# The sinks' share of windowed attention: two float32 products a pair of heads, or one float32r product in high and low parts

## The chip, the cores and the metric

One core of a Trainium2 chip runs the whole program; times are device microseconds (us). Five engines work side by side and meet through semaphores: TensorE (PE, with its weight loads PEld), VectorE (DVE), ScalarE (ACT), GpSimd (POOL) and SyncE (SP), which issues most DMAs. Each runs its own instructions in order. The metric is the time of one execution; the median of 3 runs of the kernel before is 604.55 us (604.28 to 604.63).

## The reference, cut to what matters

```python
# B, H, S, D = 2, 8, 768, 64;  n_sink = 4, window = 128
scores = scale * q @ k.T                       # per batch and head
keep = (key < n_sink) | (0 <= query - key < window)
a = softmax(where(keep, scores, -1e9))
x = (a @ v)  ->  [B*S, H*D] = [1536, 512]      # this is the attention
x = gate1(x @ w_in1) @ w_out1                  # 512 -> 2048 -> 512
x = gate2(x @ w_in2) @ w_out2
```

A query sees the 128 keys of its window and the first 4 keys of the sequence, the sinks. Results are wanted in float32.

## The kernel before, in words

The kernel first computes the attention and then the two feed-forward layers. `GROUPS` cuts the 1536 rows into four groups of (chunk, batch, first query block, number of blocks): (0,0,0,4), (1,0,4,2), (1,1,0,2), (2,1,2,4). Each group is gone through for 4 pairs of heads, which makes 16 pairs of 2 or 4 *units* (a unit is one block of 128 queries for both heads of the pair, 48 in all).

`score` multiplies q and k into PSUM (`ps_s`, L435), DVE adds the mask and takes the row's extreme (L448), ACT takes the exponential and its sum (`sm`, L484). `normalise` runs once for two units: DVE forms 1/sum (L459, L460), copies the normalised columns of the sinks into `psk` (L462; only where the sinks lie outside the window, which is so in 16 of the 24 calls), and GpSimd (L475), ACT (L477) or DVE (L479) scale the rest of `p`. `turn` transposes `p` on TensorE (L520, L521) and ACT or DVE copy it to `pt`. `sinks` transposes `psk` (L527, into `ps_k`) and DVE multiplies it by `own` into `pts` (L530), so that every block of queries keeps only its own rows. `mix` multiplies `v` with `pt` into `ps_v` (L562), for each block of keys and for both heads of the pair by turns, and in 12 of the 16 pairs adds the sinks' part: `vs` with `pts`, one float32 product for each head, last in the sum. ACT and DVE then split the sum into a high and a low part (`xh`, `xl`), since the layers that follow work in float32r with three products (high*high, high*low, low*high).

The order of the steps is written out in the list `steps`: two scores, then the two transposes of the units scored 4 units earlier, `sinks` at a pair's end and its `mix` two units later. `defer(fn, n)` puts work n steps later. PE and SP follow the program's order; on DVE and ACT a scheduler orders by priority before the run. `begin` issues the loads of the first three pairs, clears `vs`, `own` and `psk` on GpSimd and then loads `vs` from DRAM (`load_sinks`, L408): 16 DMAs of 4 KB, since `vs` holds the sinks' rows once for each of 4 query blocks (32 rows a block, 4 rows of the first head, 4 of the second). While the attention runs, pieces of the first layer's weights (float64 in DRAM) are already narrowed on DVE and ACT, and in three places the first products of the layer (`h_group`, L699) stand between attention steps.

Of the kernel before, what the change touches and what calls it, by code (L numbers as in the profile page):

```python
# [63 lines left out]
def sink_columns(n_sink):  # L64
    return n_sink + n_sink % 2


def f32(ap):
    return ap.bitcast(F32)
# [3 lines left out]
def sink_attention_moe_moe_kernel(  # L73
# [44 lines left out]
    def defer(fn, slots=1):  # L118
        waiting.append((clock[0] + slots, fn))
# [209 lines left out]


    NS = sink_columns(n_sink) if fast else 0
    KB = P + NS
    steps = []

# [11 lines left out]
    def build_fast_attention(at_p):  # L346
# [49 lines left out]
            qk[j] = (tq, tk)  # L396

        SR = P // NQ
        vs = at_p.tile([P, B, DM], F32, name="vs", bufs=1)
        pts = [at_p.tile([P, NQ, P], F32, name=f"pts{n}", bufs=1) for n in range(2)]  # L400
        psk = [at_p.tile([P, NQ, SR], F32, name=f"psk{n}", bufs=1) for n in range(DIST)]
        own = at_p.tile([P, NQ], F32, name="own", bufs=1)

        def load_sinks():
            for b in range(B):
                for e in range(2):
                    for r in range(e * NS, P, SR):
                        nc.sync.dma_start(  # L408
                            out=vs[r:r + NS, b, :].rearrange("s (h e d) -> s h e d", e=2, d=D)[:, :, e, :],
                            in_=v[b, 0:NS, :].rearrange("s (h e d) -> s h e d", e=2, d=D)[:, :, e, :],  # L410
                        )
# [13 lines left out]
        def score(j, u):  # L425
            b, i0, nq, first, nb = geom(pairs[j][0])
            tq, tk = qk[j]
            i = i0 + u
            w = widths[min(i, 2)]
            c0 = key_column(max(i - 1, 0)) - key_column(first)  # L430
            banks = []
            for e in range(2):
                rows = slice(e * D, (e + 1) * D)
                banks.append(ps_h.tile([P, 512], F32, tag="h", name="ps_s")[:, :w])
                nc.tensor.matmul(  # L435
                    banks[e], tq[rows, u * P:(u + 1) * P], tk[rows, c0:c0 + w], start=True, stop=True
                )
            if u % 2 == 0:
                two[j] = (
                    at_p.tile([P, 4, 2 * KB], F32, tag="p", name="p", bufs=DIST // 2 + 2),  # L440
                    at_p.tile([P, 4], F32, tag="nm", name="nm", bufs=DIST // 2 + 2),
                    at_p.tile([P, 4], F32, tag="sm", name="sm", bufs=DIST // 2 + 2),
                )
            p4, nm, sm = two[j]
            v = 2 * (u % 2)
            p = p4[:, v:v + 2, :w]
            for e in range(2):
                nc.vector.tensor_tensor_reduce(  # L448
                    out=p[:, e, :], in0=banks[e], in1=masks[min(i, 2)], scale=-SCALE, scalar=BIG,
                    op0=ALU.add, op1=ALU.min, accum_out=nm[:, v + e:v + e + 1],  # L450
                )
                bal.add("dve", 230 + w / 0.96)
            probs[j, u] = p
            if u == nq - 1:
                qk.pop(j)
                defer(lambda: load(j + 3))

            def normalise():
                nc.vector.tensor_scalar_add(out=sm, in0=sm, scalar1=1e-9)  # L459
                nc.vector.reciprocal(out=sm, in_=sm)  # L460
                if w > 2 * P:
                    nc.vector.tensor_tensor(  # L462
                        out=psk[j % DIST][:, u - 1:u + 1, 0:2 * NS].rearrange("p u (e s) -> p u e s", e=2),
                        in0=p4[:, :, P:KB].rearrange("p (u e) s -> p u e s", e=2),
                        in1=sm.rearrange("p (u e) -> p u e", e=2).unsqueeze(3).to_broadcast([P, 2, 2, NS]), op=ALU.mult,
                    )
                end = units.index((j, u)) >= len(units) - 4
                for x in (u - 1, u):
                    for e in range(2):
                        c = 2 * (x % 2) + e  # L470
                        px, r = probs[j, x][:, e, :], sm[:, c:c + 1]
                        if w > 2 * P:
                            px = p4[:, c].rearrange("p (n k) -> p n k", k=KB)[:, :, 0:P]
                        if c < (1 if end else 3):
                            nc.gpsimd.tensor_scalar_mul(out=px, in0=px, scalar1=r)  # L475
                        elif bal.pick(act=190 + w / 1.2, dve=150 + w / 1.4) == "act":
                            nc.scalar.activation(out=px, in_=px, func=AF.Copy, scale=r)  # L477
                        else:
# [12 lines left out]

            defer(expo)
# [31 lines left out]
        def sinks(j, us, nq):  # L524

            ps = bank("ps_k")[:, 0:P]
            nc.tensor.transpose(ps, psk[j % DIST].rearrange("p u s -> p (u s)"), ident)  # L527
            shape = [P, nq - us, P]
            with tc.high_priority(URGENT):
                nc.vector.tensor_tensor(  # L530
                    out=pt[j][1][:, us:nq, :], in0=ps.unsqueeze(1).to_broadcast(shape),
                    in1=own[:, us:nq].unsqueeze(2).to_broadcast(shape), op=ALU.mult,
                )
            bal.add("dve", 140 + (nq - us) * P / 0.96)

        def mix(j):
            gi, hp = pairs[j]
            b, i0, nq, first, nb = geom(gi)
            tv = vv.pop(j)
            ts = vs[:, b, hp * P:(hp + 1) * P]  # L540
            t, tsink = pt.pop(j)
            ps = bank("ps_v")[:, :nq * P]
            us = max(2 - i0, 0)
            sink = us < nq
            ops = [[], []]
            for e in range(2):
                cs = slice(e * D, (e + 1) * D)
                te = t[:, e].rearrange("p n k q -> p (n k q)")
                for kb in range(nb):
                    u = first + kb - i0  # L550
                    u0, u1 = max(u, 0), min(u + 1, nq - 1)
                    c0 = u0 * 2 * P + (P if u >= 0 else 0)
                    c1 = c0 + (u1 - u0 + 1) * P
                    ops[e].append((u0, u1 + 1, tv[:, kb, cs], te[:, c0:c1]))
                o = 0 if i0 == 0 else 1
                ops[e] = ops[e][o::2] + ops[e][1 - o::2]
                if sink:
                    ops[e].append((us, nq, ts[:, cs], tsink[:, us:nq, :].rearrange("p n q -> p (n q)")))
            for n in range(len(ops[0])):
                for e in range(2):  # L560
                    u0, u1, l, r = ops[e][n]
                    nc.tensor.matmul(  # L562
                        ps[e * D:(e + 1) * D, u0 * P:u1 * P], l, r, start=n == 0, stop=n == len(ops[0]) - 1
                    )
            load_v(j + 2)
            n = nq * P
            cs = slice(col0[gi], col0[gi] + n)
            xh, xl = (x_at(0, GROUPS[gi][0], part, hp)[:, cs] for part in "hl")
            with tc.high_priority(URGENT if j >= len(pairs) - 2 else 0):
                high(xh, ps, n, True)  # L570
                low(xl, ps, xh, n)
# [3 lines left out]
        def begin():  # L575
            load(0)
            load_v(0)
            load(1)
            load_v(1)
            load(2)  # L580
            with tc.manual_schedule(engines={mybir.EngineType.Pool}):
                prepare()
                make_identity(nc, ident)
                for t in (vs, own, *psk):
                    nc.gpsimd.memset(t, 0.0)
                for u in range(NQ):
                    nc.gpsimd.memset(own[u * SR:(u + 1) * SR, u:u + 1], 1.0)
            load_sinks()
# [528 lines left out]
```

## Time and profile before

| | |
|---|---|
| median of 3 runs | 604.55 us |
| the profiled execution, its own time | 603.75 us |
| its span, first to last instruction | 602.0 us |
| PE / DVE / ACT / POOL busy in the span | 98 / 78 / 65 / 18 % |
| granted TensorE clock | full in every slice |

A busy engine is one that has an instruction under way. A matmul's recorded time overlaps with that of the next, so what a matmul takes of the engine is read from start to start and not from its length. DVE and ACT overlap a little at the ends of instructions in the same way.

### The profile page before, as it was taken

The numbers are of one execution on the slowest core, as the hardware profiler recorded it, in microseconds if no ns is written. First come the engines' busy times: TensorE is split into PE (matmuls) and PEld (weight loads), VectorE is DVE, ScalarE is ACT, GpSimd is POOL, SyncE is SP. The second block draws the span as 40 slices with busy tenths as digits, with TensorE's granted clock in tenths as the row PEclk, the third lists the DMA queues.
The fourth block names the chain that finished last, engine by engine and source line by source line (L and its number), as shares of the span: only waits on it lengthen the run. The fifth ranks groups of instructions, "written<-read, shape, count | busy, mean of one in ns | idle before, by whom it ended". The sixth has DMA issues, their size and how long they took to land.

```text
span 602.0 us, 8261 instructions
## 1 busy us (share of the span) xinstructions
PE 590.9 (98%) x2872; PEld 473.4 (79%) x2872; DVE 472.3 (78%) x865; ACT 393.8 (65%) x702; POOL 109.5 (18%) x163
## 2 busy tenths in 40 slices
PE   7999899999999999999999999999999999999997
PEld 5666567887888888888888888888888888888885
DVE  5888899799788878577799898897888875666652
ACT  6888897686566665576788785565556545454442
POOL 8676741201011101110000001111011210000000
PEclk9999999999999999999999999999999999999999
DMA  4447713966567676666457105777767555964303
GB/s 143 140 115 243 265 22 106 332 222 225 160 185 235 187 232 180 186 208 234 170 183 271 72 0 175 197 223 212 207 185 235 140 168 152 326 228 139 106 1 140
DMA packets 41786, 107.63 MB, mean 179 GB/s; under 512 B 3728, under 2 KB 13968, under 8 KB 41744
## 3 DMA queue, kind: packets, MB, share of 16 engines
q1 hardware_dynamic: 29872, 72.09, 37.5%
q0 software_dynamic: 11296, 34.61, 18.9%
q8 instruction: 23, 0.38, 0.3%
q10 hardware_dynamic: 576, 0.40, 0.2%
q14 instruction: 19, 0.16, 0.1%
HBM read 69.34 MB, written 35.65 MB: 174 GB/s over the span
## 4 chain that ended last, share of the span: by engine, by line
PE 84%; DVE 7%; ACT 4%; POOL 2%; issue 1%; DMA 1%; POOLq 0%; DVEq 0%
PE ps_y L934 42%; PE ps_h L699 35%; PE ps_v L562 3%; ACT p L484 2%; PE ps_s L435 2%; POOL p L475 1%; DMA wo_d<-w 1%; PE ps_t L521 1%; DVE p L448 1%; PE ps_t L520 1%; DVE w L224 1%; DVE x L773 1%; ACT pt L502 1%; ACT w L198 0%; DVE xt L145 0%
## 5 line engine op out<-in xcount | busy, mean ns | idle before, releaser
L934 PE MATMUL ps_y<-gh,wo 128*128 128x512 f32 x768 | 241.8, 389 | 0.0
L934 PEld LDWEIGHTS ps_y<-gh,wo 128*128 128x128 f32 x768 | 144.2, 188 | 30.0
L934 PE MATMUL ps_y<-gl,wo 128*128 128x512 f32 x384 | 149.8, 390 | 0.3 <-DVE gl L145 0.2
L699 PE MATMUL ps_h<-xh,wi 128*128 128x512 f32 x432 | 140.6, 390 | 0.0
L699 PEld LDWEIGHTS ps_h<-xh,wi 128*128 128x128 f32 x432 | 81.1, 188 | 18.4 <-issue 1.6
L934 PEld LDWEIGHTS ps_y<-gl,wo 128*128 128x128 f32 x384 | 72.1, 188 | 16.4 <-DVE gl L145 1.6
L699 PE MATMUL ps_h<-xl,wi 128*128 128x512 f32 x216 | 84.2, 390 | 0.0
L475 POOL TENSOR_SCALAR p<-p,sm 128x256 f32<-128x256 f32 (+1 forms) x68 | 58.7, 877 | 25.8 <-DVE sm L460 15.7
L699 PE MATMUL ps_h<-xt,st 128*128 128x512 f32 x252 | 61.9, 389 | 0.0
L138 ACT ACTIVATE gh<-r 128x512 fp32r<-128x512 f32 x64 | 40.1, 628 | 29.8 <-PE ps_y L934 27.7
L145 DVE TENSOR_TENSOR gl<-r,gh 128x512 fp32r<-128x512 f32 x64 | 43.8, 689 | 15.7 <-ACT gh L138 15.5
L699 PEld LDWEIGHTS ps_h<-xt,st 128*128 128x128 f32 x252 | 47.2, 188 | 10.0 <-DVE hq L827 0.2
L484 ACT ACTIVATE p<-p,nm 128x260 f32<-128x260 f32 (+2 forms) x96 | 46.3, 484 | 10.8 <-DVE nm L448 10.4
L699 PEld LDWEIGHTS ps_h<-xl,wi 128*128 128x128 f32 x216 | 40.5, 188 | 8.8 <-DVE xl L145 0.4
L448 DVE CUSTOM_DVE_ANT_0 p<-ps_s,mask 128x260 f32<-128x260 f32 (+2 forms) x96 | 35.0, 397 | 6.0 <-PE ps_s L435 5.1
L714 POOL DMA_DIRECT2D h_d<-hq x32 | 18.7, 583 | 114.2 <-ACT xt L138 43.5
L679 ACT ACTIVATE r<-hq,half 128x512 f32<-128x512 f32 x32 | 22.8, 723 | 24.7 <-DVE gl L145 18.8
L272 POOL DMA_DIRECT2D wo_d<-w x16 | 8.6, 537 | 165.3 <-DVE w L224 165.3
L827 DVE TENSOR_TENSOR hq<-ps_h,p 128x512 f32<-128x512 f32 x42 | 28.9, 688 | 10.9 <-PE ps_h L699 10.8
L435 PE MATMUL ps_s<-kraw,qraw 64*128 64x260 f32 (+2 forms) x192 | 32.9, 428 | 4.3 <-DMA kraw<-k_dram 3.2
L680 DVE SCALAR_TENSOR_TENSOR r<-r,hq 128x512 f32<-128x512 f32 x32 | 21.8, 691 | 18.6 <-ACT r L679 18.5
L138 ACT ACTIVATE wo<-w 128x1024 fp32r<-128x1024 f32 (+1 forms) x17 | 17.2, 1009 | 24.4 <-DVE w L224 24.4
(109 smaller groups left out, 949.3 us busy)
## 6 DMA issues: line engine op xcount, KB each, us to landing
h_d<-hq POOLq DMA_DIRECT2D x32, 512.0 KB, 6.1
hq<-h_d SPq DMA_DIRECT2D x32, 512.0 KB
wo_d<-w POOLq DMA_DIRECT2D x16, 512.0 KB, 7.2
raw1i<-moe_w_in_dram SPq DMA_DIRECT2D x8, 1024.0 KB
wr<-wo_d SPq DMA_DIRECT2D x16, 512.0 KB
raw1o<-moe_w_out_dram SPq DMA_DIRECT2D x8, 1024.0 KB
raw0i<-moe_w_in_dram SPq DMA_DIRECT2D x7, 1024.0 KB
raw0o<-moe_w_out_dram SPq DMA_DIRECT2D x7, 1024.0 KB
```

What stands on the lines that cost most here:

```text
L138: nc.scalar.activation(out=dst, in_=src, func=AF.Copy)
L145: nc.vector.tensor_tensor(out=dst, in0=src, in1=f32(hi), op=ALU.subtract)
L435: nc.tensor.matmul(banks[e], tq[rows, u * P:(u + 1) * P], tk[rows, c0:c0 + w], start=True, stop=True)
L448: nc.vector.tensor_tensor_reduce(out=p[:, e, :], in0=banks[e], in1=masks[min(i, 2)], scale=-SCALE, scalar=BIG, op0=ALU.add, op1=ALU.min, a ...
L475: nc.gpsimd.tensor_scalar_mul(out=px, in0=px, scalar1=r)
L484: nc.scalar.activation(out=p[:, e, :], in_=p[:, e, :], func=AF.Exp, scale=-1.0, bias=nm[:, v + e:v + e + 1], accum_out=sm[:, v + e:v + e + 1],
L679: nc.scalar.activation(out=r, in_=h, func=AF.Relu, scale=1.0 / 6.0, bias=half)
L680: nc.vector.scalar_tensor_tensor(out=g, in0=r, scalar=1.0, in1=h, op0=ALU.min, op1=ALU.mult)
L699: nc.tensor.matmul(ps, a[:, kc, :], b[kc], start=start and i == 0, stop=i == len(ops) - 1, skip_group_check=not start,)
L714: nc.gpsimd.dma_start(out=h_d[m][fc // 2][:, e:e + 2, :], in_=t)
L827: nc.vector.tensor_tensor(out=dst, in0=src, in1=p1, op=ALU.add)
L934: nc.tensor.matmul(ys[dm], a[:, cs], b, start=fc == 0 and i == 0, stop=last and i == 2)
```

## The change

For the sinks, `p` and `v` are each split into a high part that float32r holds and the low rest. A head now takes 12 of its 16 rows of a query block's 32: in `psk` they hold p-high, p-low, p-high, in `vs` v-high, v-high, v-low, so that one product over the rows sums the three products. Both heads share one product of 128 columns of weights, put first in the sum of `mix`; the heads' products of `pt` follow, no longer with odd and even key blocks apart. `normalise` writes the sinks to a small tile `pss`, from which DVE makes the parts with two more instructions. `load_sinks` becomes one DMA into a staging tile `vsraw`, and 6 steps later a copy on ACT, a subtraction on DVE, 6 small DMAs from `vsraw` to `vs`, and 3 DMAs that repeat the first 32 rows.

```diff
+    split_sinks = fast and 6 * NS <= P // max(g[3] for g in GROUPS)
...
+        SH = SR // 2
+        SD = F32R if split_sinks else F32
...
+            nc.sync.dma_start(out=flat, in_=v[:, 0:NS, :].rearrange("b s f -> s b f"))
+
+            def split():
+                nc.scalar.activation(out=hi.bitcast(F32R), in_=flat, func=AF.Copy)
+                nc.vector.tensor_tensor(out=lo.bitcast(F32R), in0=flat, in1=hi, op=ALU.subtract)
+                for e in range(2):
+                    for n, part in enumerate((hi, hi, lo)):
+                        r = e * SH + n * NS
+                        nc.sync.dma_start(out=heads(f32(vs[r:r + NS]), e), in_=heads(part, e))
+                for u in range(1, NQ):
+                    nc.sync.dma_start(out=f32(vs[u * SR:(u + 1) * SR]), in_=f32(vs[0:SR]))
+
+            defer(split, 6)
...
+                    t = psk[j % DIST][:, 2 * (u - 1):2 * (u + 1), :]
+                    ts = at_p.tile([P, 4, NS], F32, tag="pss", name="pss", bufs=2) if split_sinks else t[:, :, 0:NS]
                     nc.vector.tensor_tensor(
...
+                        out=ts, in0=p4[:, :, P:KB], in1=sm.unsqueeze(2).to_broadcast([P, 4, NS]), op=ALU.mult
                     )
+                    if split_sinks:
+                        parts = t[:, :, 0:3 * NS].rearrange("p u (n s) -> p u n s", s=NS)
+                        nc.vector.tensor_copy(out=parts[:, :, 0::2, :], in_=ts.unsqueeze(2).to_broadcast([P, 4, 2, NS]))
+                        nc.vector.tensor_tensor(
+                            out=parts[:, :, 1, :], in0=ts, in1=f32(parts[:, :, 0, :]), op=ALU.subtract
+                        )
...
+                if split_sinks:
+                    continue
                 o = 0 if i0 == 0 else 1
                 ops[e] = ops[e][o::2] + ops[e][1 - o::2]
                 if sink:
                     ops[e].append((us, nq, ts[:, cs], tsink[:, us:nq, :].rearrange("p n q -> p (n q)")))
+            whole = sink and split_sinks
+            if whole:
+                nc.tensor.matmul(
+                    ps[:, us * P:nq * P], ts, tsink[:, us:nq, :].rearrange("p n q -> p (n q)"), start=True, stop=False
+                )
```

On TensorE the first `mix` of the program, that of pair 0, stands between transposes and scores. These are the rows of before.

```order
L521 MATMUL ps_t<-ident,p 128x128
L562 MATMUL ps_v<-pt,vraw 64x256 x6
L562 MATMUL ps_v<-pt,vraw 64x128 x2
L562 MATMUL ps_v<-pts_128,vs 64x256 x2
L435 MATMUL ps_s<-kraw,qraw 128x260 x4
```

These are the rows of the change at the same place.

```order
L557 MATMUL ps_t<-ident,p 128x128
L599 MATMUL ps_v<-pts_128,vs 128x256
L605 MATMUL ps_v<-pt,vraw 64x256 x6
L605 MATMUL ps_v<-pt,vraw 64x128 x2
L465 MATMUL ps_s<-kraw,qraw 128x260 x4
```

Two products of the sinks with 64 columns of weights have become one with 128, and the product with `vs` has moved from the end of the `mix` to its head.

On DVE this is the end of pair 0 and the start of pair 1, around the second call of `normalise` (`sm`), before the change.

```order
L448 ISA p,nm<-ps_s,mask_124 128x128
L448 ISA nm 128x1
L459 TENSOR_SCALAR sm<-sm 128x4
L460 RECIPROCAL sm<-sm 128x4
L462 TENSOR_TENSOR psk_130<-p,sm 128x2x8
L479 TENSOR_SCALAR p<-p,sm 128x2x128
L448 ISA p,nm<-ps_s,mask_125 128x256
```

With the change DVE holds these rows there.

```order
L478 ISA p,nm<-ps_s,mask_124 128x128
L478 ISA nm 128x1
L421 TENSOR_TENSOR vsraw<-vsraw 4x1024
L489 TENSOR_SCALAR sm<-sm 128x4
L478 ISA p,nm<-ps_s,mask_125 128x256
L478 ISA nm 128x1
L478 ISA p,nm<-ps_s,mask_125 128x256
L478 ISA nm 128x1
L490 RECIPROCAL sm<-sm 128x4
L540 COPY pt<-ps_t 128x2x128
L494 TENSOR_TENSOR pss<-p,sm 128x16
L515 TENSOR_SCALAR p<-p,sm 128x2x128
```

The subtraction of `vsraw` now stands ahead of the sum's reciprocal, and two score reductions stand between the two instructions that form it.

On ACT, the exponentials of the same units stand like this before the change.

```order
L484 ACTIVATE p,sm<-p,nm 128x256 x2
L484 ACTIVATE p,sm<-p,nm 128x260
L477 ACTIVATE p<-p,sm 128x256
L484 ACTIVATE p,sm<-p,nm 128x260 x3
L484 ACTIVATE p,sm<-p,nm 128x128 x2
```

With the change ACT holds these rows there.

```order
L520 ACTIVATE p,sm<-p,nm 128x256 x2
L520 ACTIVATE p,sm<-p,nm 128x260
L513 ACTIVATE p<-p,sm 128x256
L520 ACTIVATE p,sm<-p,nm 128x260 x2
L420 ACTIVATE vsraw<-vsraw 4x1024
L520 ACTIVATE p,sm<-p,nm 128x260
L520 ACTIVATE p,sm<-p,nm 128x128 x2
```

The copy of `vsraw` stands ahead of the last exponential of pair 0, whose sum the second `normalise` needs. On SP the change issues these DMAs at the start (before, the 16 of L408 stood between the first `kraw` and `qraw` rows).

```order
L396 DMA kraw<-k_dram 128x520
L417 DMA vsraw<-v_dram 4x2x512
L395 DMA qraw<-q_dram 128x512
L396 DMA kraw<-k_dram 128x520
L425 DMA vs<-vsraw 4x8x64 x6
L427 DMA vs<-vs 32x1024 x3
L395 DMA qraw<-q_dram 128x256
```

The staged load follows the bulk of the first three pairs' loads, and the DMAs that fill `vs` follow the loads of pair 3.

## Rows read from the trace of the kernel before

**Rows 1.** Chain that ended last, in order of time: start us, us, engine, tile, line.
```profile
149.37 0.61 DVE gl L145
149.99 0.04 issue
150.03 2.77 PE ps_y L934 x11
...
159.60 2.72 PE ps_y L934 x12
...
597.87 0.02 issue
```

**Rows 2.** The same chain, earlier.
```profile
25.50 0.28 DVE sm L459
...
35.02 1.40 PE ps_s L435 x6
...
60.38 0.27 PE ps_t L521
```

**Rows 3.** Busy time by stretch: us, then each engine's busy us (instructions), clock, DMA.
```profile
16.00:41.00 25.00, 24.43 (x187) 16.62 (x188) 21.00 (x97) 21.21 (x71) 17.83 (x21) 1.00 0.46 135
41.00:61.00 20.00, 19.79 (x178) 13.69 (x176) 16.69 (x78) 17.72 (x63) 14.10 (x19) 1.00 0.69 221
61.00:84.00 23.00, 21.05 (x160) 13.32 (x158) 20.05 (x89) 20.68 (x66) 16.81 (x18) 1.00 0.51 172
84.00:102.00 18.00, 17.62 (x112) 12.86 (x112) 16.55 (x38) 15.61 (x34) 3.06 (x4) 1.00 0.18 59
```

**Rows 4.** PE in order of time: start us, us from first start to last end.
```profile
31.42 0.60 PE L562 MATMUL ps_v<-pts,vs 128*64 128x256 f32 x4
31.95 1.15 PE L435 MATMUL ps_s<-kraw,qraw 64*128 64x260 f32 x8
...
73.42 1.03 PE L562 MATMUL ps_v<-pts,vs 128*64 128x512 f32 x4
74.38 1.15 PE L435 MATMUL ps_s<-kraw,qraw 64*128 64x260 f32 x8
```

**Rows 5.** DMA from 0 to 20 us in 40 slices of 0.5 us, GB/s.
```profile
GB/s 0 0 0 75 245 236 140 294 333 330 328 364 307 341 363 397 340 153 8 1 8 8 7 1 8 8 6 2 8 8 8 0 8 8 7 95 217 391 335 156
```

**Rows 6.** PE, ACT, DVE and POOL in order of time, at the start.
```profile
2.96 1.78 PE L435 MATMUL ps_s<-kraw,qraw 64*128 64x128 f32 x8 [2.96 <-DMA kraw<-k_dram]
...
8.71 0.50 ACT L484 ACTIVATE p<-p,nm 128x260 f32<-128x260 f32 x1
...
9.34 0.17 DVE L459 TENSOR_SCALAR sm<-sm 128x4 f32<-128x4 f32 x1 [0.61 <-ACT p L484]
9.54 0.18 DVE L460 RECIPROCAL sm<-sm 128x4 f32<-128x4 f32 x1
9.82 0.17 DVE L462 TENSOR_TENSOR psk<-p,sm 128x16 f32<-128x16 f32 x1
9.92 0.35 DVE L479 TENSOR_SCALAR p<-p,sm 128x256 f32<-128x256 f32 x1
...
9.89 5.07 POOL L475 TENSOR_SCALAR p<-p,sm 128x256 f32<-128x256 f32 x6 [0.49 <-DVE sm L460]
...
16.00 1.73 PE L562 MATMUL ps_v<-pt,vraw 128*64 128x256 f32 x16
```

**Rows 7.** Groups by form: busy us, mean ns of one; then issues of `vs`: min/median/max ns.
```profile
L145 DVE TENSOR_TENSOR xt<-x,xt 128x1024 fp32r<-128x1024 f32 x4 | 4.9, 1223 | 0.0
L138 ACT ACTIVATE xt<-x 128x1024 fp32r<-128x1024 f32 x4 | 4.2, 1059 | 0.1
...
L408 SPq DMA_DIRECT2D vs<-v_dram x16: 613/627/817, 5.7 to 15.9; - x16
```

**Rows 8.** DVE in order of time, two waits on TensorE in the last group.
```profile
75.22 0.43 DVE L448 CUSTOM_DVE_ANT_0 p<-ps_s,mask 128x260 f32<-128x260 f32 x1 [1.03 <-PE ps_s L435]
...
95.53 0.69 DVE L530 TENSOR_TENSOR pts<-ps_k,own 128x512 f32<-128x512 f32 x1 [0.40 <-PE ps_k L527]
```

More of the change, by code (lines that the diff above doesn't have):

```diff
@@ L398, in build_fast_attention, with heads, load_split_sinks @@
         SR = P // NQ
-        vs = at_p.tile([P, B, DM], F32, name="vs", bufs=1)
-        pts = [at_p.tile([P, NQ, P], F32, name=f"pts{n}", bufs=1) for n in range(2)]
-        psk = [at_p.tile([P, NQ, SR], F32, name=f"psk{n}", bufs=1) for n in range(DIST)]
-        own = at_p.tile([P, NQ], F32, name="own", bufs=1)
+        SH = SR // 2
+        SD = F32R if split_sinks else F32
+        vs = at_p.tile([P, B, DM], SD, name="vs", bufs=1)
+        pts = [at_p.tile([P, NQ, P], SD, name=f"pts{n}", bufs=1) for n in range(2)]
+        psk = [at_p.tile([P, 2 * NQ, SH], SD, name=f"psk{n}", bufs=1) for n in range(DIST)]
+        own = at_p.tile([P, NQ], F32, name="own", bufs=1)
+        def heads(t, e):
+            return t.rearrange("s b (h e d) -> s b h e d", e=2, d=D)[:, :, :, e, :]
+        def load_split_sinks():
+            t = raw_p.tile([P, 2, DM, 2] if wide else [P, 2, DM], I32 if wide else F32, tag="raw", name="vsraw")
+            t = t.rearrange("p a f w -> p (a f w)") if wide else t.rearrange("p a f -> p (a f)")
+            flat, hi = (
+                t[0:NS, n * B * DM:(n + 1) * B * DM].bitcast(F32).rearrange("s (b f) -> s b f", b=B) for n in range(2)
+            )
+            lo = flat
+            nc.sync.dma_start(out=flat, in_=v[:, 0:NS, :].rearrange("b s f -> s b f"))
[9 more added lines that the diff above has]
+            defer(split, 6)
         def load_sinks():
+            if split_sinks:
+                load_split_sinks()
+                return
             for b in range(B):
                 for e in range(2):
-                    for r in range(e * NS, P, SR):
+                    for r in range(e * SH, P, SR):
                         nc.sync.dma_start(
@@ L461, in normalise @@
                 if w > 2 * P:
+                    t = psk[j % DIST][:, 2 * (u - 1):2 * (u + 1), :]
+                    ts = at_p.tile([P, 4, NS], F32, tag="pss", name="pss", bufs=2) if split_sinks else t[:, :, 0:NS]
                     nc.vector.tensor_tensor(
-                        out=psk[j % DIST][:, u - 1:u + 1, 0:2 * NS].rearrange("p u (e s) -> p u e s", e=2),
-                        in0=p4[:, :, P:KB].rearrange("p (u e) s -> p u e s", e=2),
-                        in1=sm.rearrange("p (u e) -> p u e", e=2).unsqueeze(3).to_broadcast([P, 2, 2, NS]), op=ALU.mult,
-                    )
+                        out=ts, in0=p4[:, :, P:KB], in1=sm.unsqueeze(2).to_broadcast([P, 4, NS]), op=ALU.mult
+                    )
+                    if split_sinks:
[4 more added lines that the diff above has]
+                        )
                 end = units.index((j, u)) >= len(units) - 4
@@ L526, in sinks @@
             ps = bank("ps_k")[:, 0:P]
-            nc.tensor.transpose(ps, psk[j % DIST].rearrange("p u s -> p (u s)"), ident)
+            nc.tensor.transpose(ps, f32(psk[j % DIST].rearrange("p u s -> p (u s)")), ident)
             shape = [P, nq - us, P]
@@ L554, in mix @@
                     ops[e].append((u0, u1 + 1, tv[:, kb, cs], te[:, c0:c1]))
+                if split_sinks:
+                    continue
                 o = 0 if i0 == 0 else 1
@@ L558, in mix @@
                     ops[e].append((us, nq, ts[:, cs], tsink[:, us:nq, :].rearrange("p n q -> p (n q)")))
+            whole = sink and split_sinks
+            if whole:
+                nc.tensor.matmul(
+                    ps[:, us * P:nq * P], ts, tsink[:, us:nq, :].rearrange("p n q -> p (n q)"), start=True, stop=False
+                )
             for n in range(len(ops[0])):
@@ L562, in mix @@
                     nc.tensor.matmul(
-                        ps[e * D:(e + 1) * D, u0 * P:u1 * P], l, r, start=n == 0, stop=n == len(ops[0]) - 1
+                        ps[e * D:(e + 1) * D, u0 * P:u1 * P], l, r, start=n == 0 and not whole,
+                        stop=n == len(ops[0]) - 1,
                     )
@@ L584, in begin @@
                 for t in (vs, own, *psk):
-                    nc.gpsimd.memset(t, 0.0)
+                    nc.gpsimd.memset(t.bitcast(F32), 0.0)
                 for u in range(NQ):
```

## The prediction

> **What bounds the kernel now.** I read the chain that ended last first. From 150.03 us to 597.87 it is TensorE alone, at 2.72 us for 12 products, 0.227 us each [rows 1]. Nothing of the change lies there, so the end moves by as much as the work at 150 us moves. What released TensorE at 150.03 was DVE's low part `gl`, begun at 149.37 [rows 1]: behind the attention TensorE and DVE are level, and an earlier TensorE gains nothing if DVE is not earlier too. All of the question is therefore what the change does to the attention, the first 102 us, on DVE and ACT as well as on TensorE.
>
> In the attention the chain changes its engine. Until 35.02 us it goes to and fro between ACT's exponentials and DVE (a piece of it is DVE's `sm` at 25.50); from 35.02 to 60.38 it is TensorE's products and transposes one after the other; behind that it passes from DVE and GpSimd to TensorE and back [rows 2]. The busy times say the same: from 41 to 61 us TensorE is busy 19.79 of 20 us, and ACT 17.72 and DVE 16.69 of it are not far below; from 84 to 102 DVE is busy 16.55 of 18 [rows 3].
>
> **What the sinks' products give back.** The four recorded products with 256 columns (two heads, two records each) start at 31.42 and the next scores at 31.95: 0.53 us of TensorE. With 512 columns it is 74.38 less 73.42, 0.96 us [rows 4]. A float32r product over 512 columns takes 0.227 us [rows 1]. None with 256 columns is in the trace: it costs at least half of that, 0.11, and at most what the float32 ones cost, 0.53. I take 0.13, by the row of its own type. So 0.40 us is saved in each of the eight 256-column `mix`es and 0.73 in each of the four with 512: 8 x 0.40 + 4 x 0.73 = 6.1 us of TensorE. What of it counts is read stretch by stretch.
>
> Up to 35 us two and a half of the eight lie in a chain that does not go through `mix` but through ACT and DVE [rows 2]. I count nothing. From 35.02 to 60.38, where the chain is TensorE, five `mix`es with sinks stand: 5 x 0.40 = 2.0 us. ACT has 20 - 17.72 = 2.3 us of idle time in the 20 us from 41 and DVE 3.3 [rows 3], so they can follow most of the way, not all: **-1.6 us** (from -2.1 to -0.5, the last if the 256-column product is dear).
>
> In the last group (61 to 101 us) four `mix`es save 0.73 each, 2.9 us. DVE and GpSimd set the pace there, and what they can have of it are DVE's waits for TensorE: 1.03 us at 75.22 for the scores behind a `mix`, of which one shorter `mix` gives 0.73, and 0.40 at 95.53 [rows 8]. That is -1.1. Against it stand DVE's new instructions.
>
> **What DVE gets in addition.** Two instructions in each of 16 `normalise` calls, 32 in all. None of this shape is in the trace; the nearest is L462. It lasts 0.17 us, but the next instruction starts 0.10 after it (9.82 to 9.92) where it needs nothing of it, and L462 itself starts 0.28 after L460 (9.54), and L460 0.20 after L459 (9.34), where each needs the last one's result [rows 6]. A new instruction so costs 0.10 to 0.28 us, 3.2 to 9 us in sum. In half of the calls the scheduler has put other work between them, so I take 0.14 on average, 4.5 us. Most of it hides in DVE's waits: in the first two groups, and in the last one until 75.22, DVE waits for ACT or TensorE shortly behind each call. Three calls lie behind 75.22, where DVE is nearly full (16.55 of 18 [rows 3]): 6 x 0.14 = +0.8. With the -1.1 the last group gives **-0.3 us** (from -1.3, all found in waits, to +0.6, at 0.28 each).
>
> The Trainium skill has a rule for this in "VectorE: DVE Perf Modes", section "The DRAIN you can't avoid": the next op does not start until the pipe is empty, and a semaphore between ops costs nothing extra. The trace differs on both counts: a next instruction starts before the last one ends, and one that waits starts later than one that doesn't. By the rule each new instruction would cost its 0.17 us wherever it stands, 5.4 us in sum.
>
> **What the start pays.** ACT's copy of `vsraw` has the form of a 128x1024 copy to float32r, 1.06 us, and DVE's subtraction of one with 1.22 us [rows 7]; 4 partitions or 128 take the same, I suppose, since the columns are as many. Both stand in the way of the exponentials and of `normalise` of pair 0. The staged load is issued behind the bulk of the first loads, which flow until about 8.7 us [rows 5]. The first loads flow from 1.5 us [rows 5], and TensorE can begin at 2.96 [rows 6], so I let `vsraw` be there at 9.2, half a microsecond behind the bulk (an estimate). ACT comes to its copy at 8.71 [rows 6], waits until 9.2 and is done at 10.3. DVE subtracts from 10.3 to 11.5, and its L459, at 9.34 before [rows 6], comes 2.2 us later. Two score reductions (0.43 each [rows 8], overlapping a little) now stand in front of the reciprocal: GpSimd starts its six scalings at 12.5 instead of 9.89, and, at 5.07 us for all six, ends at 17.6 instead of 14.96. Before, the first `mix` came 1 us behind that, at 16.00 [rows 6]; now it can come at 18.1 to 18.6.
>
> It begins with the sinks, so it needs `vs`: six DMAs from 10.3 on, 0.63 us to issue each [rows 7], until 14.1; 1.5 to 2 us to land (estimated from the 1.5 us between the first flow and TensorE's start), then three more and another landing: about 19. The first `mix` comes 3 us late and, being 0.4 shorter, ends 2.6 late. DVE and ACT lose less, since the scores of the units before lie ready: at least the 1.06 us put into ACT, at most the whole 3.0. I take **+1.75 us**, between the bound and the 2.6. The chain from there to 35 us has no room to make it good. That 16 DMA issues of 0.63 us are gone from SP gives nothing: TensorE waits for no load between the first scores and 60 us that these hold up.
>
> **The sum.** +1.75 - 1.6 - 0.3 = -0.15 us. The profiled execution's own time is 603.75, so 603.6; the median of the runs stands 0.8 above that execution, which makes 604.4.
>
> **The rivals.**
> *The start is cheap and TensorE's saving pays.* `vsraw` comes early and `vs` in time: +1.0; all of the 35 to 60 stretch, -2.1, and -1.3 in the last group. Sum -2.4, 602.1. For it: the long stretch in which only TensorE is in the chain. Against it: ACT's 17.72 of 20 us. Chance 0.31.
> *The start is dear.* `vs` comes after two DMA hops only past 20 us, and the `mix` that waits for it now does so at its head, with the next scores queued behind it on TensorE. From a landing at 20.5 on DVE and ACT run dry too: +3.0; with -1.2 from 35 to 60 and nothing in the last group, +1.8, 606.3. Chance 0.20.
> *DVE becomes the bound.* The new instructions, at 0.24 each because each needs the one ahead, in the 11 calls outside the TensorE stretch: 22 x 0.24 = 5.3 us, half of it outside waits, +2.6. It decides when DVE no longer waits at 75.22 and 95.53. Sum +1.75 - 1.6 + 2.6 = +2.75, 607.3. For it: DVE's 16.55 of 18 us; against it the 3.3 us free from 41 to 61. By the skill's rule above the same 22 would cost 3.7 us instead of 5.3. Chance 0.11.
> *No change to speak of*, the forecast: 0.38.
>
> **How the numbers follow.** 0.2%, 1.2 us, is what a measurement of this kernel tells from no change. The first rival is faster by more (0.31), the next two slower (0.31), the forecast within (0.38). The forecast's own range is 603.3 to 605.7; since cases of both signs hold most of the chance, the range reaches from a little below the first rival to between the other two: 602.0 to 606.9.
>
> **What would show it.** In the changed profile: ACT's copy of `vsraw` near 9.2 us and DVE's subtraction near 10.3; the first `mix` at 18 to 19.5 behind a wait for the DMA of `vs`; the sinks' product taking 0.1 to 0.15 us of TensorE to the next start with 256 columns and 0.23 with 512; TensorE's chain from 35 to 60 some 1.6 us shorter, with ACT almost without gaps; DVE without the waits at 75 and 95; and the first products behind 150 us, in equal rhythm, moved by the sum alone. The prediction fails if the start is made good before 35 us, if ACT can't follow TensorE, or if DVE's new instructions push the sums that GpSimd waits for.

## The result and the profile after

The changed kernel takes 609.71 us (median of 6 runs, 607.82 to 610.75), the kernel before, run beside it, 604.41. The ratio is 1.0086, with a 95% interval of 1.0074 to 1.0099: slower by 5.3 us, outside the predicted range. The profiled execution took 608.61 us with a span of 606.8, 4.8 more than the span of before.

The chain that ended last begins in the new start. These are pieces of it in order of time (start, duration, what; SPq is SyncE issuing a DMA; line numbers are those of each kernel's own file).

```profile
1.65 3.58 DMA kraw<-k_dram
5.25 4.77 DMA vsraw<-v_dram
10.04 1.06 ACT vsraw L420
11.12 1.21 DVE vsraw L421
...
14.82 1.97 DMA vs<-vsraw
17.00 0.59 SPq L427
17.65 0.58 SPq L427
18.27 2.59 DMA vs<-vs
...
134.53 2.81 PE ps_y L978 x11
```

The small load is issued at 5.25 and there at 10.02; copy, subtraction and two DMA hops follow one another until 20.86 us. Before, DVE formed 1/sum at 9.34 and 9.54 and GpSimd began its six scalings at 9.89 [rows 6]. These are DVE's rows of the same place now, then the scalings in GpSimd's timeline.

```profile
11.12 1.21 DVE L421 TENSOR_TENSOR vsraw<-vsraw 4x1024 fp32r<-4x1024 f32 x1 [2.11 <-ACT vsraw L420]
12.27 0.15 DVE L489 TENSOR_SCALAR sm<-sm 128x4 f32<-128x4 f32 x1
12.34 0.41 DVE L478 CUSTOM_DVE_ANT_0 p<-ps_s,mask 128x256 f32<-128x256 f32 x1
...
12.68 0.41 DVE L478 CUSTOM_DVE_ANT_0 p<-ps_s,mask 128x256 f32<-128x256 f32 x1
...
13.03 0.16 DVE L490 RECIPROCAL sm<-sm 128x4 f32<-128x4 f32 x1
```

```profile
13.35 5.09 POOL L511 TENSOR_SCALAR p<-p,sm 128x256 f32<-128x256 f32 x6 [3.64 <-DVE sm L490]
```

DVE stood 2.11 us behind the copy, two score reductions came in between, and GpSimd waited 3.64 us for the reciprocal. TensorE transposes what GpSimd scaled; rows of its timeline until the first `mix`:

```profile
16.43 0.48 PE L556 MATMUL ps_t<-ident,p 128*128 128x128 f32 x1 [0.21 <-DVE nm L478]
...
16.91 0.42 PE L556 MATMUL ps_t<-ident,p 128*128 128x128 f32 x1
17.12 0.42 PE L557 MATMUL ps_t<-ident,p 128*128 128x128 f32 x1
17.34 0.42 PE L563 MATMUL ps_k<-ident,psk 128*128 128x128 f32 x1
17.69 1.65 PE L465 MATMUL ps_s<-kraw,qraw 64*128 64x128 f32 x8
19.27 0.69 PE L557 MATMUL ps_t<-ident,p 128*128 128x128 f32 x2
...
19.94 0.27 PE L557 MATMUL ps_t<-ident,p 128*128 128x128 f32 x1
20.05 0.27 PE L556 MATMUL ps_t<-ident,p 128*128 128x128 f32 x1
...
21.00 0.35 PE L599 MATMUL ps_v<-pts,vs 128*128 128x256 f32 x1 [0.57 <-DMA vs<-vs]
```

Rows of the same timeline before:

```profile
10.21 0.42 PE L520 MATMUL ps_t<-ident,p 128*128 128x128 f32 x1
10.42 0.42 PE L521 MATMUL ps_t<-ident,p 128*128 128x128 f32 x1
...
12.83 0.33 PE L520 MATMUL ps_t<-ident,p 128*128 128x128 f32 x1
...
13.52 1.62 PE L435 MATMUL ps_s<-kraw,qraw 64*128 64x128 f32 x8
15.07 0.44 PE L521 MATMUL ps_t<-ident,p 128*128 128x128 f32 x2
...
15.56 0.27 PE L520 MATMUL ps_t<-ident,p 128*128 128x128 f32 x1
15.67 0.27 PE L521 MATMUL ps_t<-ident,p 128*128 128x128 f32 x1
```

The first `mix` begins at 21.00 instead of 16.00 [rows 6], only 0.57 us of it a wait for `vs`. Equal transposes follow each other at 0.21 us in the changed kernel until 17.34 and at 0.11 from 19.94; before, the 0.21 ended with 10.42, and from 12.53 on they stood at 0.11. The rest of the story is in four places of each profile: the start of the first and of the last of the 16 `mix`es (the TensorE timeline), the start of the last `pts` on DVE (its timeline), and the span. Those of the experiments, told below, stand here too; "time" is the median of the runs, all else is read from one profiled execution each, and "middle" is last less first.

| kernel | time | first mix | last mix | middle | last pts | span |
|---|---|---|---|---|---|---|
| before | 604.55 | 16.00 | 98.17 | 82.17 | 95.53 | 602.0 |
| changed | 609.71 | 21.00 | 102.48 | 81.48 | 99.93 | 606.8 |
| e1 start undone | 606.07 | 18.48 | 100.01 | 81.53 | 97.46 | 604.7 |
| e2 no parts | 607.35 | 20.49 | 101.50 | 81.01 | 98.94 | 604.6 |
| e3 product alone | 604.55 | 18.40 | 99.10 | 80.70 | 96.54 | 604.2 |
| e4 start in before | 608.33 | 20.79 | 102.61 | 81.82 | 99.96 | 606.6 |
| e5 operations only | 608.56 | 20.77 | 102.48 | 81.71 | 99.84 | 606.1 |
| e6 hops only | 606.20 | 16.02 | 100.64 | 84.62 | 98.00 | 604.3 |
| e7 early | 606.12 | 17.88 | 99.56 | 81.68 | 97.00 | 603.7 |
| e8 product, GpSimd spared | 604.37 | 16.57 | 97.35 | 80.78 | 94.80 | 602.2 |
| e9 the same with parts | 605.05 | 17.10 | 98.55 | 81.45 | 95.99 | 603.4 |
| e10 no sinks' product | 602.70 | 16.72 | 96.59 | 79.87 | 93.95 | 601.1 |
| e11 early and small | 605.19 | 17.60 | 99.32 | 81.72 | 96.76 | 603.6 |

So the changed kernel starts its `mix`es 5.0 us late, makes good 0.7 of it until the last, and ends 4.8 late. One execution is not another: e10 has the same start as before, yet its first `mix` came 0.7 us later (16.72 against 16.00), so a smaller difference in that column between two rows says nothing by itself.

The new products in TensorE's timeline, one of 256 and one of 512 columns, each with the row that starts next (PEld rows are weight loads):

```profile
53.61 0.19 PEld L599 LDWEIGHTS ps_v<-pts,vs 128*128 128x128 f32 x1 [0.61 <-PE ps_k L563]
53.64 0.35 PE L599 MATMUL ps_v<-pts,vs 128*128 128x256 f32 x1 [0.40 <-DVE xl L145]
53.92 0.85 PEld L605 LDWEIGHTS ps_v<-pt,vraw 128*64 128x64 f32 x12
...
83.50 0.47 PE L599 MATMUL ps_v<-pts,vs 128*128 128x512 f32 x1
83.90 1.71 PEld L605 LDWEIGHTS ps_v<-pt,vraw 128*64 128x64 f32 x20 [0.24 <-issue]
```

From start to start it is 0.28 us with 256 columns (0.28 to 0.32 over the eight) and 0.40 with 512, where 0.53 and 0.96 stood [rows 4] and I had 0.13 and 0.23. The saving is 8 x 0.25 + 4 x 0.56 = 4.2 us of TensorE, not 6.1. The next weights begin to load only where the next product starts, 0.31 us after this one's load began. That would fit a load of 0.19 us that is not hidden behind products as short as these, but no run tested it. The Trainium skill says in "TensorE: Matmul & The Clock Gate", section "Back-to-back issue gap", that the spacing of products is set by the weight load and the product together; the trace fits it, with 0.28 us from start to start above the load's 0.19. By that page's formulas, one laid behind the other (0.107 for 128 columns of weights, from its section "LDWEIGHTS (loading the stationary operand)", and 0.109 for a product of 256 columns at full clock) it would be an estimated 0.22 us, against 0.28 measured.

### The profile page after: what moved, and what is told of

It reads as the page before. It is cut to its first block, busy times and chain, and to the rows that moved or that the text cites. A ratio compares the mean times of both kernels' runs of the same rounds, so it can differ in the third digit from the quotient of the medians.

```text
span 606.8 us, 8226 instructions
## 1 busy us (share of the span) xinstructions
PE 591.1 (97%) x2836; PEld 473.8 (78%) x2836; DVE 478.9 (79%) x898; ACT 394.8 (65%) x703; POOL 109.0 (18%) x163
## 4 chain that ended last, share of the span: by engine, by line
PE 83%; DVE 5%; ACT 4%; DMA 4%; POOL 2%; issue 1%; SPq 0%; ACTq 0%; POOLq 0%; DVEq 0%
PE ps_y L978 42%; PE ps_h L743 36%; ACT p L520 2%; PE ps_v L605 2%; PE ps_s L465 2%; DMA wo_d<-w 1%; POOL p L511 1%; DVE p L478 1%; DMA vsraw<-v_dram 1%; PE ps_t L557 1%; DVE xl L145 1%; PE ps_t L556 1%; DMA kraw<-k_dram 1%; ACT pt L538 1%; DVE w L224 0%
## 5 line engine op out<-in xcount | busy, mean ns | idle before, releaser
L978 PEld LDWEIGHTS ps_y<-gl,wo 128*128 128x128 f32 x384 | 72.1, 188 | 17.2 <-DVE gl L145 2.2
L465 PE MATMUL ps_s<-kraw,qraw 64*128 64x260 f32 (+2 forms) x192 | 34.4, 445 | 4.1 <-DMA kraw<-k_dram 3.3
L138 ACT ACTIVATE wo<-w 128x1024 fp32r<-128x1024 f32 (+1 forms) x17 | 17.2, 1009 | 21.1 <-DVE w L224 21.1
```

The lines of the kernel that those rows point to most:

```text
L138: nc.scalar.activation(out=dst, in_=src, func=AF.Copy)
L465: nc.tensor.matmul(banks[e], tq[rows, u * P:(u + 1) * P], tk[rows, c0:c0 + w], start=True, stop=True)
L978: nc.tensor.matmul(ys[dm], a[:, cs], b, start=fc == 0 and i == 0, stop=last and i == 2)
```

## The experiments

Theory "start": the loss is the late start, and all else comes to about nothing. Rival "DVE": the 32 new instructions are the loss. A third question was why TensorE's saving did not show. e1 to e4 shared one run of the kernel before (604.20), e5 to e8 (604.06) and e9 to e11 (604.45) too.

**e1, start undone.** In the changed kernel:

```diff
+                    nc.gpsimd.dma_start(out=heads(vs[e * SH:e * SH + NS, rows], e), in_=heads(vd[:, rows], e))
...
-            defer(split, 6)
+            defer(spread, 6)
```

> The changed kernel without its start: v's four sink rows go straight from DRAM into vs, rounded on the way by four small DMAs of GpSimd, and are repeated by the same three DMAs; no vsraw, no copy on ACT, no subtraction on DVE, and the rows of v-low stay zero (v's low part is left out). All else is as in the change, with the 32 new DVE instructions. Theory 'start': the changed kernel's first mix begins 5.0 us later than before (21.00 against 16.00 us) and its end stands 4.8 us later, so this kernel begins its first mix near 16 us and ends at 604 to 606 us, 4 to 5 us under the change. Rival 'DVE': the 32 instructions are the loss, then it stays above 607.5 us though the first mix is early.

Measured: 606.07 us, 3.6 under the change, ratio to before 1.0031 (1.0020 to 1.0042). "DVE" falls as the whole of the loss. The first `mix` came at 18.48, not near 16: the four DMAs took GpSimd until 9.11, its scalings of `p` began at 9.19 instead of 7.29 (its timeline), TensorE was busy only 2.3 of the 4 us from 8 to 12, and then ran at a granted clock of 0.50.

**e2, no parts.**

```diff
-                    ts = at_p.tile([P, 4, NS], F32, tag="pss", name="pss", bufs=2) if split_sinks else t[:, :, 0:NS]
+                    ts = t[:, :, 0:NS]
...
-                        parts = t[:, :, 0:3 * NS].rearrange("p u (n s) -> p u n s", s=NS)
-                        nc.vector.tensor_copy(out=parts[:, :, 0::2, :], in_=ts.unsqueeze(2).to_broadcast([P, 4, 2, NS]))
-                        nc.vector.tensor_tensor(
-                            out=parts[:, :, 1, :], in0=ts, in1=f32(parts[:, :, 0, :]), op=ALU.subtract
-                        )
```

> The changed kernel without the 32 new DVE instructions: normalise writes the sinks' p straight into psk as its high part (p's low part is left out). The start is that of the change. Theory 'start': the first mix still begins near 21 us, and the time falls by no more than 1 us, to 608.5 to 609.7. Rival 'DVE': it falls by 3 us or more, to 604 to 606.5.

Measured: 607.35, 2.4 under the change: more than "start" allowed, less than "DVE" asked. 0.51 of it lies ahead of the first `mix` (20.49), 0.47 in the middle, and 1.2 behind the last `pts`, in the stretch in which TensorE waits for DVE (below). Of the 0.51, 0.33 stood already at the subtraction of `vsraw` (10.79 against 11.12 on DVE), ahead of the first of the 32 instructions, and so is not theirs.

**e3, product alone**: the edits of e1 and e2 together.

> Both together: the one float32r product for both heads, without the start of the change and without the 32 DVE instructions (the low parts of v and p are left out). It is what TensorE's saving alone is worth against the kernel before. In the changed kernel's profile the product of 256 columns takes 0.28 us to the next start and that of 512 columns 0.40, against 0.53 and 0.96 for the products that they replace: 8 x 0.25 + 4 x 0.56 = 4.2 us of TensorE. Theory 'a part counts': 1 to 2.5 us faster than before, 602 to 603.4. Rival 'ACT and DVE set the pace': no difference from before, 603.9 to 605.

Measured: 604.55 (602.67 to 608.27 in 12 runs), ratio 1.0013 (1.0000 to 1.0026). The rival holds. But its first `mix` still came at 18.40, behind a granted clock of 0.50 from 12 to 16 us, so it was not yet the product alone; e8 mends that.

**e4, start in before.** In the kernel before, with the rows of `vs` at `(2 * n + e) * NS` to fit its `psk`:

```diff
-                        nc.sync.dma_start(
-                            out=vs[r:r + NS, b, :].rearrange("s (h e d) -> s h e d", e=2, d=D)[:, :, e, :],
...
+            load_split_sinks()
```

> The kernel before with only the start of the change: vsraw, the copy on ACT, the subtraction on DVE, six and three DMAs into vs (the rows of the high part that psk's unchanged columns meet; the rows of the low parts meet zeros). The sinks' products are before's, last in each mix. Theory 'start': the first mix's sinks wait for vs until about 20.8 us, and the kernel ends 3.5 to 5 us later than before, 608 to 609.5. Rival: the place at the head of the mix is what makes the wait dear; last in the mix it costs 1.4 us less, 606.5 to 607.5. Rival 'DVE': the start is made good, under 606.

Measured: 608.33, ratio 1.0065 (1.0052 to 1.0078). The start by itself costs the kernel before 4.1 us. The first `mix` came as late (20.79) with the sinks last in it, so their place at its head is not what costs the most.

**e5, operations only, and e6, hops only.** In the kernel before, e5 adds to its 16 loads

```diff
+            nc.sync.dma_start(out=flat, in_=v[:, 0:NS, :].rearrange("b s f -> s b f"))
...
+                nc.scalar.activation(out=hi.bitcast(F32R), in_=flat, func=AF.Copy)
+                nc.vector.tensor_tensor(out=flat.bitcast(F32R), in0=flat, in1=hi, op=ALU.subtract)
```

and e6 replaces the 16 loads by `vsraw`'s load and

```diff
+                        r = (2 * n + e) * NS
+                        nc.sync.dma_start(out=heads(vs[r:r + NS], e), in_=heads(flat, e))
+                for u in range(1, NQ):
+                    nc.sync.dma_start(out=vs[u * SR:(u + 1) * SR], in_=vs[0:SR])
```

> The kernel before with its own 16 loads of vs, and beside them only vsraw's load, the copy on ACT and the subtraction on DVE 6 steps later (nothing uses their results). The run with the whole start in the kernel before began its first mix at 20.79 us against 16.00, GpSimd's six scalings at 13.29 against 9.89. Theory 'operations': DVE's sm waits behind the subtraction, which waits for the copy, which waits for vsraw; the scalings start near 13 us, the first mix at 19 to 20.5, the time is 606.5 to 608.5. Rival 'hops': the two chained DMAs are what the first mix waits for, then this kernel begins it by 17.5 us and stays under 605.5.

> The kernel before with vs loaded through vsraw by six and three DMAs, without the copy and the subtraction (the rows that meet psk's columns hold v itself). Theory 'operations': the scalings start at 10 us as before, and only the sinks' products, last in the first mix, wait for the second hop at 19 to 20.5 us. Theory 'hops': that wait holds the next scores on TensorE as long as the operations do, so the loss is not a sum of the two but the later one of both: 606 to 608. If DVE and ACT have scores enough in hand, it stays under 605.5 and the operations alone are the loss.

Measured: e5 608.56, ratio 1.0068 (1.0056 to 1.0081); e6 606.20, ratio 1.0034 (1.0022 to 1.0045). The two operations alone cost 4.5 us, the hops alone 2.1, both in e4 4.1: not a sum but the later of the two. In e5's profile TensorE's granted clock fell to 0.50 from 14 to 20 us, in e4's it read 1.00; so a part of e5's 4.5 may be the clock's. In e5 GpSimd's scalings start late, in e6 they do not, and only the sinks' products wait. GpSimd's timeline of e5:

```profile
13.46 6.09 POOL L490 TENSOR_SCALAR p<-p,sm 128x256 f32<-128x256 f32 x7 [4.11 <-DVE sm L475]
```

GpSimd's and TensorE's timelines of e6:

```profile
9.91 2.88 POOL L490 TENSOR_SCALAR p<-p,sm 128x256 f32<-128x256 f32 x3 [0.50 <-DVE sm L475]
```

```profile
16.02 1.73 PE L577 MATMUL ps_v<-pt,vraw 128*64 128x256 f32 x16
20.28 0.74 PE L577 MATMUL ps_v<-pts,vs 128*64 128x256 f32 x4 [2.52 <-DMA qraw<-q_dram]
20.95 0.49 PE L450 MATMUL ps_s<-kraw,qraw 64*128 64x260 f32 x2
```

The trace names `qraw` as what ended e6's wait; the last DMA into `vs` is the nearer guess, since these products read only `vs` and `pts`: it was issued at 17.32, and with the 2.8 us to landing (median of the three) it would be there at 20.1. The next scores, at 20.95 instead of 18.10 [rows 6], are 2.85 us late, of which 2.1 reach the end.

**e7, early.** The change whole, its start moved.

```diff
-            defer(split, 6)
+            defer(split, 1)
...
         def begin():
+            load_sinks()
             load(0)
...
-            load_sinks()
```

> The changed kernel whole, with its start moved: vsraw is the first load on SP, and the copy and the subtraction come one step later, ahead of the first exponentials and the first score reductions, which wait for q and k at that time. Theory 'start' (late operations and hops): copy at 3 to 4 us, subtraction until 5.5, the six DMAs at 6 to 10, vs complete near 16; first mix at 17 to 17.7 instead of 21.0, time 605 to 606.5. Rival: the 1 us in front of the first exponentials is carried along and TensorE stays at its lower clock for longer, then 607 to 609.

Measured: 606.12, ratio 1.0029 (1.0017 to 1.0041), 3.6 under the change; copy at 3.43, subtraction at 4.52, first `mix` at 17.88. All the work is done, only earlier.

**e8, product with GpSimd spared.** As e3, with

```diff
+            fetch(0)
+            defer(lambda: spread(0), 6)
+            defer(lambda: fetch(1), 40)
...
+            nc.vector.memset(vs.bitcast(F32), 0.0)
...
-                for t in (vs, own, *psk):
+                for t in (own, *psk):
```

> The one float32r product without the start and without the 32 DVE instructions again (low parts left out), now without the four DMAs of GpSimd ahead of its scalings: DVE clears vs before its first work, GpSimd issues two DMAs for batch 0 at the start and two for batch 1 later. In the run before it GpSimd's first scalings came at 9.19 us instead of 7.29, TensorE ran dry and its granted clock fell to 0.50 from 10 to 18 us; the first mix came at 18.40. Theory 'clock and start': first mix at 16 to 16.8, granted clock 1.00 throughout, time 602 to 603.5, since from the first mix to the last that run took 80.70 us against 82.17 before. Rival: the product's saving does not reach the end, 604 to 605.

In the run GpSimd issued all four DMAs early, at 2.27 and 4.07 us, between its masks. Measured: 604.37, ratio 1.0003 (0.9994 to 1.0012), with the first `mix` at 16.57 and a granted clock of 1.00 throughout. The place of its first `mix` was as the theory said, its time as the rival: the product alone gives nothing that can be measured.

**e9, the same with the 32 instructions**: e8 without the edit of e2.

> The run with the product alone and GpSimd spared (604.37), with the 32 DVE instructions put back (p's low part is there, v's is left out): the difference of the two is the price of these instructions with an undisturbed start. Two pairs so far: 609.71 less 607.35 is 2.4, 606.07 less 604.55 is 1.5 us, both with TensorE's clock lowered at the start in some executions. Theory 'DVE sets the pace of the last group and behind it': 605.2 to 606.3, with the last pts about 1 us later than in the run without. Rival 'hidden in waits', as the prediction had most of it: under 605.

Measured: 605.05, ratio 1.0015 (1.0003 to 1.0026), 0.7 above e8 by the two ratios, whose intervals overlap, and 1.2 by the last `pts`, of which 0.5 stands ahead of the first `mix`. It falls between the two expectations. In the middle, behind the first `mix`, the three pairs with and without these instructions agree: 0.5 (change and e2), 0.8 (e1 and e3) and 0.7 us.

**e10, no sinks' product in the kernel before.**

```diff
-                if sink:
-                    ops[e].append((us, nq, ts[:, cs], tsink[:, us:nq, :].rearrange("p n q -> p (n q)")))
```

> The kernel before without the sinks' products in mix (they are left out; psk, its transposes and pts stay). TensorE saves 8 x 0.53 + 4 x 0.96 = 8.1 us, twice what the float32r product saves, and no other engine has more or less to do. Theory 'given back behind the attention': the last mix comes 2 to 3 us earlier, but the chain behind it passes through DVE, a load and DVE's narrowing of the weights, TensorE waits 1 us or more between 100 and 135 us, and the time falls by 1 to 2.5 us, to 601.5 to 603. Rival 'TensorE counts': 599.5 or less, since half of 8.1 us or more reaches the end.

Measured: 602.70, ratio 0.9975 (0.9965 to 0.9985). 8.1 us taken from TensorE are worth 1.75 (0.9 to 2.1 by the interval). The middle is 2.3 us shorter of the 7.1 that stood in it (8 x 0.53 and 3 x 0.96; the fourth is the last `mix` itself), and behind the attention TensorE waits. Its waits in e10 from 96 to 152 us (total, times, longest):

```profile
PE ps_y L932 <- DVE gl L145: 1.3, 1, 1.3
PE ps_h L697 <- DVE xl L145: 0.9, 1, 0.9
```

Before, the only such wait from 98 to 152 us is 0.2 us.

**e11, early and small.** As e7, with `vsraw` over 16 partitions by 256 columns:

```diff
+                nc.sync.dma_start(out=flat[:, b, :], in_=v[b, 0:NS, :].rearrange("s (h f) -> (s h) f", f=P))
...
+            defer(split, 1)
+            defer(lambda: place(0), 3)
+            defer(lambda: spread(0), 6)
+            defer(lambda: place(1), 40)
+            defer(lambda: spread(1), 60)
```

> The changed kernel whole, with vsraw loaded first and laid out over 16 partitions by 256 columns instead of 4 by 1024, so that the copy and the subtraction are shorter, and with the DMAs into vs for batch 0 at the start and for batch 1 later. In the run with the early start the copy took 1.06 and the subtraction 1.36 us and the first mix began at 17.88. Theory: 0.4 to 0.6 us each now, first mix at 16.4 to 17.2, time 604.8 to 605.8; no faster than before, since the 32 DVE instructions remain. Rival: the first reductions wait for q and k anyway, then no gain on the run with the early start, 606.

Measured: 605.19, ratio 1.0016 (1.0007 to 1.0025). Copy and subtraction took 0.41 us each, as expected, but the first `mix` came at 17.60, not before 17.2: the load in two pieces held up q, and TensorE's first scores came at 4.01 instead of 2.96 [rows 6]. It is the fastest version of the whole change by its median (its interval and e7's overlap), still 0.7 us behind before. No run pointed to one that beats before with the whole computation.

## Why the prediction was wrong

**The start (+1.75 us) failed, twice.** The first step was its length: the first `mix` at 19, measured 21.00. `vsraw` landed at 10.02 instead of 9.2, and so the reciprocal came at 13.03 and the scalings began at 13.35 instead of 12.5, 3.46 later than before. From there to where the `mix` could have begun (20.43) it took 7.08 us, against 6.11 before, and the wait for `vs` added the last 0.57: 3.46 + 0.97 + 0.57 = 5.0. The landings were not what I had wrong there: counted as in the prediction, from the end of the last issue, they took 1.34 and 2.01 us against 1.5 to 2. `vs` came at 20.86 because the hops began 0.85 late and their six issues took 4.30 us instead of 3.8, and because my terms add up to 19 to 20, not to "about 19". The 0.97 I had not seen: 0.80 of it lies in eleven transposes of that stretch (16.43 to 17.69 and 19.27 to 20.43, against 12.83 to 13.52 and 15.07 to 16.00 before), which stood 0.21 us apart for most of it instead of 0.11. TensorE's slower pace is the likely cause and was not tested by itself.

The second step was the size of what is carried on. I let DVE and ACT lose less than the `mix` did, "since the scores of the units before lie ready". They lost nearly as much: the second `mix` is 4.4 us late (27.34 against 22.91), and e4 and e5 show 4.1 and 4.5 us at the end, where +1.75 stood in the sum. The two operations stand in a chain that ran without slack: `vsraw`, copy, subtraction, 1/sum, GpSimd's scaling, transpose. The prediction had followed this chain as far as the first `mix` (scalings at 12.5, `mix` at 19) and then let DVE and ACT make good a third of the delay out of scores in hand; there was no such reserve. What failed is that discount.

**The 35 to 60 us stretch (-1.6) gave -0.5.** Ahead of it, where I counted nothing, the way from the first `mix` to the fourth took 20.99 us instead of 21.48, another -0.5. From the fourth `mix` to the tenth it is 20.09 us (41.99 to 62.08) against 20.58 (37.48 to 58.06). I had named the case, "if the 256-column product is dear": it costs 0.28 instead of 0.13. Without DVE's new instructions e8 takes 19.65 there, -0.9, of the 5 x 0.25 = 1.25 that TensorE saved.

**The last group (-0.3) gave +0.45.** From the eleventh `mix` (65.96) to the last `pts` (99.93) it is 33.97 us against 33.52. The -1.1 of DVE's waits was not found at all: e8 takes 33.63. (The terms give -1.1 at most; the bound of -1.3 had no term behind it.) The +0.8 for DVE's instructions was about right: e9 takes 34.50, 0.87 more than e8.

**Behind the attention** I let the end move by as much as the work at 150 us. That holds for a delay, not for a gain. The way from the last `pts` goes through DVE's `w` and the DMA into `wo_d` to DVE's chain of weights, without TensorE; pieces of the changed kernel's chain:

```profile
99.93 0.70 DVE pts L566
100.63 0.69 DVE w L224
...
106.71 8.72 DMA wo_d<-w
...
133.88 0.61 DVE gl L145
```

Its busy times by stretch (us, PE, PEld, DVE, ACT, POOL busy, granted clock, DMA share, GB/s), then those of before:

```profile
106.00:120.00 14.00, 13.34 (x59) 10.73 (x58) 10.45 (x14) 8.09 (x11) 3.55 (x6) 1.00 0.97 311
120.00:135.00 15.00, 13.84 (x61) 11.15 (x61) 15.00 (x19) 11.48 (x15) 1.96 (x3) 1.00 0.86 283
```

```profile
106.00:120.00 14.00, 14.00 (x64) 11.58 (x63) 10.33 (x13) 8.92 (x10) 3.34 (x4) 1.00 1.03 331
120.00:135.00 15.00, 14.92 (x66) 12.04 (x65) 15.00 (x19) 12.87 (x17) 1.07 (x2) 1.00 0.68 233
```

DVE is busy all of 120 to 135 us, in both kernels, and TensorE idles 1.8 of the 29 us, against 0.1 before. A TensorE that is freed in the attention waits here: e8 (0.69) and e10 (1.32 of the 15 us from 120) show the same, while e4 and e5, which are as late as the change but have the old products, let it idle 0.45 and 0.01 of the 29 us. A part of the product's saving goes here: from the last `pts` to the end e8 takes 0.9 and e10 0.7 us more than before. The larger part does not reach the last `mix` at all: e8's middle is 1.4 us shorter, of the 3.7 that its products save in it.

**The rivals.** "The start is dear" had the sign and came nearest in the hop's time (I had 20.5, the trace 20.86). Its mechanism, the wait for `vs` at the head of the `mix`, was the smaller part: e6 prices the hops at 2.1, e5 the operations, which I had taken for cheap, at 4.5. "DVE becomes the bound" was the second cause, not the first: taking the 32 instructions out gave 2.4 us in the changed kernel (e2), 1.5 between e1 and e3 and 0.7 between e8 and e9, the last not clear of noise. The first two pairs have executions in which TensorE's granted clock fell in the start (to 0.57 from 16 to 20 us in e2's profile); why their price is higher is not shown. The start by itself (e4, 4.1), the product (e8, nothing that can be measured) and these instructions (0.7 to 2.4) together make 4.8 to 6.5 of the 5.3 measured.

What stays open: the median of the change lies 1.1 us above its profiled execution. Its two runs with a mean granted clock of 0.991 and 0.993 took 610.7, the other four 607.8 to 609.9; no trace shows where the clock fell in them.

## What to carry to other kernels

A small preparation put into the start is not priced by its length but by what stands behind it: follow the copied tile's landing, the engine that waits for it, and everything in that engine's queue, above all what feeds a third engine. Load such data first and do its work while the engines still wait for the first inputs; that alone gave back 3.6 of 5.3 us here. Before counting on a faster product, take the old one out altogether: the 8.1 us that left TensorE were worth 1.75, and a faster form of those products had no more than that to give in this kernel.

## What the hardware showed that I had not expected

**TensorE's clock can fall after a thin stretch.** In e5 TensorE was busy 1.79 of the 4 us from 10 on and waited 2.21 of them for DVE; then the granted clock fell to 0.50, 1.2 of 2.4 GHz, in these windows (columns as above):

```profile
10.00:14.00 4.00, 1.79 (x9) 0.88 (x8) 2.77 (x11) 3.41 (x11) 0.54 (x1) 0.96 0.03 6
14.00:18.00 4.00, 2.83 (x12) 1.60 (x11) 3.63 (x15) 2.40 (x9) 4.00 (x6) 0.50 0.09 15
18.00:22.00 4.00, 4.00 (x26) 2.81 (x28) 2.86 (x14) 3.24 (x11) 3.57 (x5) 0.68 0.87 272
```

The Trainium skill says in "TensorE: Matmul & The Clock Gate", section "What's actually happening", that the throttled state is the default and activity releases it; these windows agree. A thin stretch does not always do it: in e6 TensorE was busy 1.73 of the 4 us from 16 on, behind the wait of 2.52 shown above, and the granted clock read 1.00 throughout. In the changed kernel's profile the transposes until 17.34 stood 0.21 us apart, just as e1's at a granted 0.50, in windows whose granted clock reads 1.00; so the column doesn't tell all, and the pitch of equal products must be read beside it.

**Some of DVE's small instructions last longer while GpSimd works.** The new copy `psk` (L499) and subtraction (L500) in two places of DVE's timeline of the changed kernel:

```profile
44.42 0.42 DVE L499 CAST psk<-pss 128x32 fp32r<-128x32 f32 x1
44.88 0.41 DVE L500 TENSOR_TENSOR psk<-pss,psk 128x16 fp32r<-128x16 f32 x1
...
95.84 0.16 DVE L499 CAST psk<-pss 128x32 fp32r<-128x32 f32 x1
...
96.52 0.16 DVE L500 TENSOR_TENSOR psk<-pss,psk 128x16 fp32r<-128x16 f32 x1
```

At 44 us GpSimd scales `p` (its instructions from 42.83 run for 5.59 us), at 96 it is idle. Five of the 16 copies take 0.34 us or more, all of them while GpSimd works. The Trainium skill's "SBUF — State Buffer", section "SBUF: two separate sides", has GpSimd and some DVE instructions lock a shared pair of ports for a whole instruction. The trace bears that out in part: three of the five copies end within 0.04 us of the end of a GpSimd instruction (28.88, 44.84 and 79.02 against 28.86, 44.81 and 78.99), two end in the midst of one, and other copies took 0.17 us while GpSimd was at work. The cause stays open.
